# A spectral layer and an MLP on one core: order of the small work in the front, of two spectral stages, and of the residuals

## The chip, the cores and the metric

The kernel runs on one core of one Trainium2 chip. TensorE multiplies matrices into PSUM; VectorE, ScalarE and GpSimd work beside it, each through its own instruction queue in program order; SyncE (SP) issues the DMAs. The metric is the device time of one execution in microseconds, as the median of several runs.

## The reference, cut to what matters

```python
def _layernorm(x, axis=-1, eps=1e-5):
    m = jnp.mean(x, axis=axis, keepdims=True)
    v = jnp.var(x, axis=axis, keepdims=True)
    return (x - m) / jnp.sqrt(v + eps)

# A: x (1, 2048, 512) bf16, w_r and w_i (2048, 257)
X = rfft2(x.astype(float32)) * (w_r + 1j * w_i)
y = irfft2(X, s=(2048, 512)).astype(bfloat16)

# B: w1 (512, 1792), w2 (1792, 512)
h = einsum("bsd,df->bsf", x, w1) + b1
r = where(h > 0, h, 0)
out = einsum("bsf,fd->bsd", r * r, w2) + b2

x = A_x
h = x + A(_layernorm(x), A_w_r, A_w_i)
h2 = h + B(_layernorm(h), B_w1, B_b1, B_w2, B_b2)
```

## The kernel before

The 2048 rows of x lie as 128 partitions by 16 groups (row 16p + g is partition p, group g), a tile of 512 columns for each group. The two-dimensional transform is done with matrix multiplications by tables of sines and cosines that the kernel makes itself: integer angles by `iota` and multiply-add on GpSimd and VectorE, wrapped by reading the low 16 bits, then `Sin` on ScalarE.

*Layer norm and stage 1 (to about 23 us).* The mean drops out and the scale of a row is folded into the table: `ln1_stats(g)` takes BATCH_NORM_STATS2 and BATCH_NORM_AGGREGATE of group g on VectorE (L219, L222); `ln1_sums(g)` does the same for groups 3, 7 and 11 with two ScalarE activations and their accumulator reads (L211); `ln1_rstd(a, b)` makes the reciprocal root on GpSimd, an add and a POW (L225, L226); `ln1_fold(a, b)` multiplies the table KF by it, one VectorE instruction for each group (L230). `stage1(g0)` multiplies two groups by their folded tables (eight matmuls, L247 and L249) and copies the PSUM result into Bt, on ScalarE (L257), or, for the last three pairs (`split`), half on ScalarE and half on VectorE (L254). The optional number in `stage1(g0, n)` is a count of matmuls of ones (`warm`, L262) ahead of it.

*Tables.* fiE[0] holds angles of the second transform (9 x 128), fiE[1] the same plus a quarter turn, made on GpSimd by one instruction of 1152 elements (L286). `table_e(0)` and `table_e(1)` are the sines of both (L198), 9 blocks each, in EF[:, k, 0] and EF[:, k, 1]. fiG (`L282`, `L284`, and `angles_g`, L194) are the angles of stage 2's table GF. The inverse tables EI are transposes of EF blocks: `transposed(o, ks)` (L267) with the identity `ident` as the moving matrix, `table_i` copies them on ScalarE (L274), `table_neg` negates on VectorE (L277). The blocks 0 and 8 and KF are transposed into the free half of the first PSUM tile of the last stage-1 pair (`tr08`). `ident` is made on GpSimd by a MEMSET and an AFFINE_SELECT (L315, L316), behind the second gather.

*Weights of the spectrum.* WB[0] and WB[1] hold w_r and w_i; 9 of 16 row blocks come by plain DMA, the other 7, in reversed order, by an indirect DMA that GpSimd issues (`w_reversed(i)`, L157). The loads of W1, W2, b1 and b2 (L324, on SP) wait until both of these gathers have landed.

*Stages 2 to 4 (23 to 53 us).* The work is done for eight pairs of spectral rows. `stage2(pr)`: eight matmuls with GF (L352), copied by ScalarE into U (L368); the first two pairs go in halves (`stage2_one`, L361). `stage3(pr)`: matmuls of U with EF. Pairs 1, 3, 5 and 7 yield AB (L407, ScalarE), from which VectorE makes X by a sum and a difference (`butterfly`, L416, L417); pairs 2, 4 and 6 (`ON_PE`) do that on TensorE too and yield X directly (L398, ScalarE); pair 0 yields X in two halves (L383). `spectral(pr)`: VectorE multiplies X by the weights (L426), adds and subtracts to Z and M (L431, L432, L441, L443), and does the butterfly of the next pair between. `stage4(pr)`: matmuls of Z or M with EI, copied to T2 (L480, L477, L478). All of stages 1 to 4 share one PSUM pool, tag "mm", of four buffers of two banks.

*Stage 5 and the MLP (from 53 us).* `s5(g)` is the last transform of group g (L555), with a copy of the odd half on ScalarE (L558); `s5b(g)` makes R by an add and a subtract on VectorE (L564, L565); `s6(g)` multiplies R by KI (L574) and VectorE adds the row of x (L575, the residual hs); `s6b(g)` takes the statistics of hs, on VectorE (L589, L590) or ScalarE (L586). After `rstd`, `norm` and the transposes (`transp`, L627, L631, L633) a chunk of two to four groups goes through the MLP: `up` (L672, ReLU L675, square L676) and `down` (L705, bias and residual L709, last group L695). While chunk c is in the MLP, `prep_steps(c + 1)` lists the steps of the next chunk with due times; `run` puts each step into the program after the MLP slot at which its due time is reached. Steps of the same round (s6, s5, s5b, s6b) are due within 0.1 of each other. The PSUM banks of p5, p6 and p7 are three, tag "pp".

At the end `pin` fixes the order on every engine as the program text has it.

Of the kernel before, what the change touches and what calls it, by code (L numbers as in the profile page):

```python
# [15 lines left out]
P = 128  # L16
# [18 lines left out]
def kernel(  # L35
# [120 lines left out]
    def w_reversed(i):  # L156
        return nc.gpsimd.indirect_dma_start(  # L157
            out=WB[i][:, 9:16, :].rearrange("p j l -> p (j l)"), out_offset=None,
            in_=(A_w_r, A_w_i)[i].rearrange("k l -> (k l)").unsqueeze(1), element_offset=9 * Df,
            in_offset=bass.IndirectOffsetOnAxis(ap=idxR[:, 0:1], axis=0))  # L160
# [5 lines left out]
    nc.gpsimd.memset(identW[:], 0.0)  # L166
    nc.gpsimd.affine_select(out=identW[:], in_=identW[:], compare_op=ALU.not_equal,
                            fill=1.0 / WSC, base=0, pattern=[[-1, P]], channel_multiplier=1)

    nc.vector.tensor_single_scalar(pI[:, 1:2], pI[:, 0:1], 3, ALU.arith_shift_right)  # L170
    nc.vector.tensor_single_scalar(pI[:, 2:3], pI[:, 0:1], 7, ALU.bitwise_and)
# [41 lines left out]
    def ln1_stats(*mine):  # L213
        sts = {}
        for k in range(len(mine) + 1):
            if k < len(mine):
                g = mine[k]
                sts[g] = st = fwd.tile([P, 6], FP32, tag="st", bufs=4, name="st")
                nc.vector.bn_stats(st[:], xs[:, g, :])  # L219
            if k > 0:  # L220
                g = mine[k - 1]
                nc.vector.bn_aggr(mv1[:, g, :], sts.pop(g)[:])  # L222
# [5 lines left out]
    def ln1_fold(a, b, eng=nc.vector):  # L228
        for g in range(a, b):
            eng.tensor_scalar(KFr[:, g, :], KF[:], rs1[:, g:g + 1], None, ALU.mult)  # L230
# [45 lines left out]
    def table_neg(ks):  # L276
        nc.vector.tensor_scalar(EI[:, ks[0]:ks[-1] + 1, 2, :], EI[:, ks[0]:ks[-1] + 1, 0, :], -1.0, None, ALU.mult)  # L277

    for g in (3, 7, 11):
        ln1_sums(g)  # L280
    ln1_stats(0, 1)
# [1 line left out]
          "the angles of the first stage first")  # L283
    nc.gpsimd.tensor_scalar(fiG[:, 256:512], idxL[:, 256:512], cols[:, 0:1], float(HT), ALU.mult, ALU.add)  # L284
    ln1_rstd(0, 2)
    nc.gpsimd.tensor_scalar(fiE[1][:], fiE[0][:], 1.0, float(QT), ALU.mult, ALU.add)  # L286
    ln1_stats(2, 4)
    ln1_fold(0, 2)
    stage1(0, 14)
    ln1_stats(5)  # L290
    ln1_rstd(2, 6)
    ln1_stats(6, 8)
    ln1_fold(2, 6)
    gathers = [w_reversed(0)]
    stage1(2, 4)
    stage1(4)
    table_e(1)
    ln1_stats(9)
    ln1_rstd(6, 10)
    ln1_stats(10, 12)  # L300
    ln1_rstd(10, 12)
    angles_g(1)
    ln1_fold(6, 10)
    stage1(6, 3)
    ln1_stats(13)
    ln1_rstd(12, 14)
    sin_of(GF[:].rearrange("p t c -> p (t c)"), fiG[:])
    ln1_fold(10, 12)
    stage1(8)
    ln1_stats(14, 15)  # L310
    nc.vector.tensor_scalar(rs1[:, 14:16], mv1[:, 14:16, 1], EPS, None, ALU.add)
    nc.gpsimd.tensor_tensor(rs1[:, 14:16], rs1[:, 14:16], mhalf[:, 0:2], ALU.pow)
    ln1_fold(12, 14)
    gathers.append(w_reversed(1))
    nc.gpsimd.memset(ident[:], 0.0)  # L315
    nc.gpsimd.affine_select(out=ident[:], in_=ident[:], compare_op=ALU.not_equal,  # L316
                            fill=1.0, base=0, pattern=[[-1, P]], channel_multiplier=1)
    stage1(10, split=True)
    ln1_fold(14, 16)
    for k, (dst, src) in enumerate(((W1[:], B_w1.rearrange("(c p) f -> p c f", p=P)),  # L320
                                    (W2[:], B_w2.rearrange("(i p) d -> p i d", p=P)),
                                    (b1b[:], B_b1.rearrange("(i p) -> p i", p=P)),
# [17 lines left out]

    def cos_negs():
        nc.vector.tensor_scalar(Cn[:], EF[:, ON_PE[0]:ON_PE[-1] + 1:ON_PE[1] - ON_PE[0], 1, :], -1.0, None, ALU.mult)


    GFv = GF[:].rearrange("p t (r e j) -> p t r e j", r=2, e=2)
# [139 lines left out]

    new_u(0)
    new_u(1)
    stage2_one(0, 0, nc.scalar.copy)
    stage2_one(0, 1, nc.vector.tensor_copy)
    stage2_one(1, 0, nc.scalar.copy)  # L490
    nc.vector.tensor_copy(EI[:, 0::8, 0:2, :], tr08[:, 0:4 * P].rearrange("p (a k b) -> p a k b", a=2, k=2))
    cos_negs()
    stage3(0)
    stage2_one(1, 1, nc.scalar.copy)
    stage3(1)
    stage2(2)
    tr = mm_tile("ptr", BF16)
    transposed(tr, (1, 2, 3))
    table_i(tr, (1, 2, 3))
    stage3(2)  # L500
    for pr in range(9):
        if pr + 3 < 8:
            stage2(pr + 3)
        if 0 < pr and pr + 2 < 8:
            stage3(pr + 2)
        if pr == 7:
            warm(mm_tile("idle")[:, 0:512], 3)
        if pr > 0:
            stage4(pr - 1, split=(pr == 8))
        if pr == 8:  # L510
            warm(mm_tile("idle")[:, 0:512], 3)
        if pr == 1:
            table_neg((1, 3))
        if pr == 3:
            table_neg((4, 7))
            nc.vector.tensor_scalar(EN[:].rearrange("p n (k b) -> p n k b", k=2), EI[:, NO_M[0]:NO_M[-1] + 1, 0:2, :],
                                    -1.0, None, ALU.mult)
        if pr == 0:
            spectral(0, first_tables)
        elif pr < 8:  # L520
            spectral(pr)
        if pr == 1:
            tr = mm_tile("ptr", BF16)
            transposed(tr, (4, 5, 6, 7))
            table_i(tr, (4, 5, 6, 7))
        if pr == 5:
            sin_of(GI[:].rearrange("p t c -> p (t c)"), fiI[:])
            nc.gpsimd.tensor_copy(b1f[:], b1b[:])
        if pr == 6:
            nc.scalar.activation(junk1[:], eps[:], ACT.Sqrt, bias=eps[:])  # L530
# [14 lines left out]
    def bank(name, tag, bufs, dt=FP32):  # L545
        return ps.tile([P, 2048 // mybir.dt.size(dt)], dt, tag=tag, name=name, bufs=bufs)

    Rs = {}

    def s5(g, ahead=False):  # L550
        pe = bank("p5", "po", 2) if ahead else bank("p5", "pp", 3)
# [15 lines left out]
    def s6(g):  # L567
        py = bank("p6", "pp", 3)
        if g == 0:
            nc.tensor.matmul(py[:], lhsT=identW[:], rhs=xs[:, 0, :], start=True, stop=False)  # L570
            nc.tensor.matmul(py[:], lhsT=KI[:], rhs=Rs.pop(g)[:], start=False, stop=True)
            nc.scalar.activation(hs[:, 0, :], py[:], ACT.Copy, scale=WSC, accum_out=mv2[:, 0, 0:1])
            return
        nc.tensor.matmul(py[:], lhsT=KI[:], rhs=Rs.pop(g)[:], start=True, stop=True)  # L574
        nc.vector.scalar_tensor_tensor(hs[:, g, :], py[:], WSC, xs[:, g, :], ALU.mult, ALU.add)  # L575

    def s6b(g, on_act=False):
        if g == 0:
# [56 lines left out]
    def prep_steps(c, total):  # L635

        a, b = CHUNKS[c]
        n = b - a
        first = 2 if c == 1 else 0
        end = total - 7.3  # L640
        t0 = 1.2 if c == 1 else total - 0.5 - 2.0 * n - 7.0
        gap = (end - t0) / (n + 1 - first)
        t0 = end - (n + 1) * gap
        steps = []
        for k in range(first, n + 2):
            t = t0 + k * gap
            if k >= 2:
                steps.append((t, 0.22, lambda g=a + k - 2: s6(g)))
            if k < n:
                steps.append((t, 0.44, lambda g=a + k: s5(g)))  # L650
            if 1 <= k <= n:
                steps.append((t + 0.1, 0, lambda g=a + k - 1: s5b(g)))
            if k >= 2:
                steps.append((t + 0.1, 0, lambda g=a + k - 2: s6b(g, on_act(c, g))))
        t = t0 + (n + 1) * gap
        steps.append((t + 1.6, 0, lambda: rstd(c)))
        steps.append((t + 2.2, 0, lambda: norm(c)))
        steps.append((total - 2.4, 0.12 * n, lambda: transp(c, 0)))
        steps.append((total - 1.7, 0.12 * n, lambda: transp(c, 1)))
        return steps  # L660
# [80 lines left out]
    s6(0)  # L741
    s6b(0, True)
    s6(1)
    s6b(1)
    rstd(0)
    norm(0)
# [37 lines left out]
```

## Time and profile before

| what | value |
|---|---|
| median of 14 runs | 179.05 us (177.5 to 180.16) |
| profiled execution: its time, and its span | 177.51 us, 175.7 us |
| granted TensorE clock, mean | 1.000 |
| busy: TensorE, VectorE, ScalarE, GpSimd | 159.0, 127.2, 105.9, 37.2 us |
| last Bt copy of stage 1 ends, stage 2 goes on | 23.18, 23.24 us |
| rows of x landed (groups 0-1, 2-3, 4-7, 8-11, 12-15) | 3.66, 5.18, 6.62, 9.55, 10.81 us |
| gathers landed | 15.50, 23.23 us |

In the profile's lines PE is TensorE, PEld its weight load, DVE VectorE, ACT ScalarE, POOL GpSimd. Times are from the start of the span in microseconds. A line of the chain gives a start, a duration and what was done; the chain is followed back from the last instruction to what released each step. A line of the waits names who waited for whom, the total, the number of times and the longest. In the timeline, an instruction is overlapped by the next of its engine, so a step from one start to the next is shorter than the duration that stands there. The 14 runs lie at three levels, 177.5 (three runs), 178.7 to 179.1 (five) and 180.0 to 180.2 (six).

### The profile page before, as it was taken

The numbers are of one execution on the slowest core, as the hardware profiler recorded it, in microseconds if no ns is written. First come the engines' busy times: TensorE is split into PE (matmuls) and PEld (weight loads), VectorE is DVE, ScalarE is ACT, GpSimd is POOL, SyncE is SP. The second block draws the span as 40 slices with busy tenths as digits, with TensorE's granted clock in tenths as the row PEclk, the third lists the DMA queues.
The fourth block names the chain that finished last, engine by engine and source line by source line (L and its number), as shares of the span: only waits on it lengthen the run. The fifth ranks groups of instructions, "written<-read, shape, count | busy, mean of one in ns | idle before, by whom it ended". The sixth has DMA issues, their size and how long they took to land.

```text
span 175.7 us, 2735 instructions
## 1 busy us (share of the span) xinstructions
PE 159.0 (91%) x995; PEld 92.9 (53%) x995; DVE 127.2 (72%) x297; ACT 105.9 (60%) x184; POOL 37.2 (21%) x65
## 2 busy tenths in 40 slices
PE   3878487999998899989999999999999998999992
PEld 1355355787865476556544544544544453556461
DVE  6999768889975688759888476488757558468231
ACT  3979456899897376078752577454277523568300
POOL 8769740000000000525000054000025200025000
PEclk9999999999999999999999999999999999999999
DMA  5983259940000000010000100000100000010011
GB/s 150 302 299 103 59 147 407 331 34 0 2 0 0 4 0 0 32 35 0 0 0 30 63 0 0 2 30 30 34 30 0 0 30 4 30 60 0 0 50 45
DMA packets 7918, 10.29 MB, mean 59 GB/s; under 512 B 2272, under 2 KB 6368, under 8 KB 7904
## 3 DMA queue, kind: packets, MB, share of 16 engines
q1 hardware_dynamic: 7744, 9.19, 16.8%
q0 software_dynamic: 160, 0.92, 1.8%
q8 instruction: 8, 0.13, 0.3%
q14 instruction: 6, 0.05, 0.1%
HBM read 8.01 MB, written 2.10 MB: 58 GB/s over the span
## 4 chain that ended last, share of the span: by engine, by line
PE 65%; DVE 18%; ACT 7%; POOL 5%; issue 3%; POOLq 0%; ACTq 0%; DVEq 0%
PE ph L672 26%; PE po L705 24%; DVE st L219 2%; PE p L555 2%; DVE KFr L230 2%; PE p L574 2%; DVE hs L575 2%; PE p L627 2%; PE po L693 2%; ACT U L368 2%; POOL rs L226 2%; PE p L352 2%; ACT rl L675 1%; DVE R L564 1%; DVE R L565 1%
## 5 line engine op out<-in xcount | busy, mean ns | idle before, releaser
L672 PE MATMUL ph<-UT,W 128*128 128x384 bf16 (+2 forms) x280 | 49.9, 336 | 1.2 <-ACT UT L631 1.0
L675 ACT ACTIVATE rl<-ph,b1f 128x384 bf16<-128x384 f32 (+2 forms) x70 | 41.5, 602 | 13.9 <-PE ph L672 10.2
L705 PE MATMUL po<-W,act 128*128 128x512 bf16 x210 | 49.1, 379 | 0.0
L676 DVE TENSOR_TENSOR act<-rl 128x384 bf16<-128x384 bf16 (+2 forms) x70 | 34.2, 514 | 16.2 <-ACT rl L675 15.7
L679 POOL TENSOR_TENSOR hb<-hs,b2b 128x512 f32<-128x512 bf16 x16 | 18.4, 1153 | 105.8 <-DVE act L676 105.8
L672 PEld LDWEIGHTS <-W 128*128 128x128 bf16 x280 | 27.4, 98 | 22.6 <-issue 1.7
L705 PEld LDWEIGHTS <-act 128*128 128x128 bf16 x210 | 20.4, 98 | 21.8 <-issue 0.6
L709 DVE TENSOR_TENSOR ot<-po,hb 128x512 bf16<-128x512 f32 x15 | 10.3, 688 | 9.4 <-PE po L705 8.2
L575 DVE SCALAR_TENSOR_TENSOR hs<-p,xs 128x512 bf16<-128x512 f32 x15 | 10.3, 684 | 2.4 <-PE p L574 2.4
L558 ACT COPY od<-p 128x256 f32<-128x256 f32 x16 | 5.9, 371 | 9.1 <-PE p L555 8.9
L631 ACT COPY UT<-p 128x768 bf16<-128x768 bf16 (+2 forms) x5 | 4.2, 842 | 11.0 <-PE p L627 11.0
L262 PE MATMUL p<-ones 128*128 128x512 bf16 x21 | 6.8, 478 | 2.9 <-POOL ones L153 2.9
L555 PE MATMUL p<-GI,T 128*128 128x256 bf16 x64 | 9.1, 272 | 0.2 <-DVE T L478 0.2
L352 PE MATMUL p<-GF,Bt 128*128 128x256 bf16 x64 | 8.3, 273 | 0.5 <-DVE Bt L254 0.3
L555 PEld LDWEIGHTS <-T 128*128 128x128 bf16 x64 | 6.2, 97 | 4.5 <-issue 1.4
L219 DVE BATCH_NORM_STATS2 st<-xs 128x6 f32<-128x512 bf16 x13 | 8.5, 677 | 0.0
L586 ACT ACTIVATE junk<-hs 128x512 bf16<-128x512 bf16 x6 | 3.8, 630 | 7.7 <-DVE hs L575 7.7
L262 PEld LDWEIGHTS <-ones 128*128 128x128 bf16 x39 | 4.2, 109 | 7.6 <-POOL ones L153 2.9
L564 DVE TENSOR_TENSOR R<-p,od 128x256 bf16<-128x256 f32 x16 | 6.7, 416 | 2.1 <-ACT od L558 2.1
L574 PE MATMUL p<-R,KI 128*128 128x512 bf16 x15 | 5.7, 381 | 1.6 <-DVE R L565 1.6
L480 ACT CAST T<-p 128x1024 bf16<-128x1024 f32 x7 | 7.2, 1027 | 0.0
L352 PEld LDWEIGHTS <-Bt 128*128 128x128 bf16 x64 | 6.1, 98 | 1.8 <-ACT Bt L254 0.5
(171 smaller groups left out, 230.9 us busy)
## 6 DMA issues: line engine op xcount, KB each, us to landing
W<-in_B_w_dram SPq DMA_DIRECT2D x2, 1792.0 KB, 9.8
out_dram<-ot SPq DMA_DIRECT2D x15, 128.0 KB, 1.8
xs<-in_A_x_dram SPq DMA_DIRECT2D x3, 512.0 KB, 5.9
WB<-in_A_w_r_dram SPq DMA_DIRECT2D x1, 578.2 KB, 5.8
WB<-in_A_w_i_dram SPq DMA_DIRECT2D x1, 578.2 KB, 6.8
xs<-in_A_x_dram SPq DMA_DIRECT2D x2, 256.0 KB, 3.5
b2b<-in_B_b_dram SPq DMA_DIRECT2D x1, 128.0 KB, 9.2
out_dram<-ot SPq DMA_DIRECT2D x2, 64.0 KB, 1.5
```

The costliest lines, as they stand in the source:

```text
L219: nc.vector.bn_stats(st[:], xs[:, g, :])
L262: nc.tensor.matmul(o, lhsT=ones[:, 0:P], rhs=ones[:], start=True, stop=True)
L352: nc.tensor.matmul(puv[:, :, e, :], lhsT=Bt[:, 2 * t + 1 - e, 2 * pr + q, :], rhs=GFv[:, t, :, e, :], start=(t == 0), stop=(t == 1))
L555: nc.tensor.matmul(pe[:, 256 - 256 * e:512 - 256 * e], lhsT=T2[:, lt, g].rearrange("p q s -> p (q s)"), rhs=GI[:, lt, :], start=(r == 0), ...
L574: nc.tensor.matmul(py[:], lhsT=KI[:], rhs=Rs.pop(g)[:], start=True, stop=True)
L575: nc.vector.scalar_tensor_tensor(hs[:, g, :], py[:], WSC, xs[:, g, :], ALU.mult, ALU.add)
L672: nc.tensor.matmul(ph[:, 0:n], lhsT=W1[:, d, bass.ts(f, P)], rhs=UT[:, d, 0:n], start=(d == 0), stop=(d == ND - 1))
L675: nc.scalar.activation(rl[:, 0:n], ph[:, 0:n], ACT.Relu, bias=b1f[:, f:f + 1], scale=1.0)
L676: sq = nc.vector.tensor_tensor(act[:, f, 0:n], rl[:, 0:n], rl[:, 0:n], ALU.mult)
L679: add = nc.gpsimd.tensor_tensor(hb[:, g, :], hs[:, g, :], b2b[:], ALU.add)
L705: nc.tensor.matmul(po[:], lhsT=act[:, f, bass.ts(i, P)], rhs=W2[:, f, :], start=(f == 0), stop=(f == NF - 1))
L709: nc.vector.tensor_tensor(ot[:], po[:], hb[:, g, :], ALU.add)
```

## The change

1. `ident` is made right behind `identW`, near the start of GpSimd's queue.
2. The quarter-turn angles of fiE[1], one instruction of nine blocks, become two: `angles_c(slice(0, 9, 8))` for the blocks 0 and 8, and `angles_c(slice(1, 8))` for the seven between. Both stand later on GpSimd. `table_e(1)` becomes `table_c` of the same two pieces; the second stands behind the last pair of stage 1.
3. The first gather goes ahead of the first folds; on GpSimd it stands before the first angle piece and `ln1_rstd(2, 6)`.
4. Group 13's statistics go from VectorE to ScalarE (`ln1_sums(13)`, between the copies of pairs 0 and 2). Group 9's statistics go ahead of the folds of groups 2 to 5. The reciprocal roots are taken in groups 0-1, 2-5, 6-9, 10-13 and 14-15 (12 and 13 were on their own). The folds of 14 and 15 go ahead of the pair of groups 10 and 11. The matmuls of ones are 12, 6 and 2 (were 14, 4 and 3).
5. Of the first two halves of stage 2, VectorE copies the first and ScalarE the second (was the other way).
6. Stage 2 of pair 2 is put ahead of stage 3 of pair 1; the transposes of blocks 1 to 3 go behind stage 3 of pair 2; `table_neg((1, 3))` goes behind `spectral(1)`.
7. The residual add of `s6` becomes a step of its own, `s6a`, which is called with `s6b`; so in the rounds of `prep_steps` it stands behind `s5b`.

```diff
+    nc.gpsimd.memset(ident[:], 0.0)
+    nc.gpsimd.affine_select(out=ident[:], in_=ident[:], compare_op=ALU.not_equal,
+                            fill=1.0, base=0, pattern=[[-1, P]], channel_multiplier=1)
...
+    def angles_c(sl):
+        return nc.gpsimd.tensor_scalar(fiE[1][:].rearrange("p (a b) -> p a b", a=9)[:, sl],
+                                       fiE[0][:].rearrange("p (a b) -> p a b", a=9)[:, sl], 1.0, float(QT), ALU.mult,
+                                       ALU.add)
+
+    def table_c(sl):
+        nc.scalar.activation(EF[:, sl, 1, :], fiE[1][:].bitcast(I16)[:, ::2].rearrange("p (a b) -> p a b", a=9)[:, sl],
+                             ACT.Sin, scale=SIN_SCALE)
...
     ln1_rstd(0, 2)
-    nc.gpsimd.tensor_scalar(fiE[1][:], fiE[0][:], 1.0, float(QT), ALU.mult, ALU.add)
+    gathers = [w_reversed(0)]
     ln1_stats(2, 4)
-    ln1_fold(0, 2)
-    stage1(0, 14)
+    f01 = ln1_fold(0, 2)
+    angles_c(slice(0, 9, 8))
+    stage1(0, 12)
+    ln1_sums(13)
     ln1_stats(5)
     ln1_rstd(2, 6)
-    ln1_stats(6, 8)
+    ln1_stats(6, 8, 9)
+    ln1_rstd(6, 10)
     ln1_fold(2, 6)
-    gathers = [w_reversed(0)]
-    stage1(2, 4)
+    stage1(2, 6)
     stage1(4)
-    table_e(1)
-    ln1_stats(9)
-    ln1_rstd(6, 10)
+    table_c(slice(0, 9, 8))
     ln1_stats(10, 12)
-    ln1_rstd(10, 12)
+    ln1_fold(6, 10)
     angles_g(1)
-    ln1_fold(6, 10)
-    stage1(6, 3)
-    ln1_stats(13)
-    ln1_rstd(12, 14)
+    ln1_rstd(10, 14)
+    stage1(6, 2)
     sin_of(GF[:].rearrange("p t c -> p (t c)"), fiG[:])
+    ln1_stats(14)
+    angles_c(slice(1, 8))
     ln1_fold(10, 12)
     stage1(8)
-    ln1_stats(14, 15)
+    ln1_stats(15)
...
     ln1_fold(12, 14)
     gathers.append(w_reversed(1))
-    nc.gpsimd.memset(ident[:], 0.0)
-    nc.gpsimd.affine_select(out=ident[:], in_=ident[:], compare_op=ALU.not_equal,
-                            fill=1.0, base=0, pattern=[[-1, P]], channel_multiplier=1)
+    ln1_fold(14, 16)
     stage1(10, split=True)
-    ln1_fold(14, 16)
...
+    table_c(slice(1, 8))
...
-    stage2_one(0, 0, nc.scalar.copy)
-    stage2_one(0, 1, nc.vector.tensor_copy)
+    stage2_one(0, 0, nc.vector.tensor_copy)
+    stage2_one(0, 1, nc.scalar.copy)
...
     stage2_one(1, 1, nc.scalar.copy)
+    stage2(2)
     stage3(1)
-    stage2(2)
+    stage3(2)
     tr = mm_tile("ptr", BF16)
     transposed(tr, (1, 2, 3))
     table_i(tr, (1, 2, 3))
-    stage3(2)
...
-        if pr == 1:
-            table_neg((1, 3))
...
         if pr == 1:
+            table_neg((1, 3))
...
-        nc.vector.scalar_tensor_tensor(hs[:, g, :], py[:], WSC, xs[:, g, :], ALU.mult, ALU.add)
+        Ys[g] = py
+
+    def s6a(g):
+        nc.vector.scalar_tensor_tensor(hs[:, g, :], Ys.pop(g)[:], WSC, xs[:, g, :], ALU.mult, ALU.add)
...
-                steps.append((t + 0.1, 0, lambda g=a + k - 2: s6b(g, on_act(c, g))))
+                steps.append((t + 0.1, 0, lambda g=a + k - 2: (s6a(g), s6b(g, on_act(c, g)))))
...
     s6(1)
+    s6a(1)
     s6b(1)
```

## The prediction

> **What bounds the kernel now.** I read the table of stretches first (length, then busy time and instruction count of TensorE, its weight loads, VectorE, ScalarE, GpSimd, then the granted clock):
>
> ```profile
> 4.40:23.20 18.80, 13.42 (x88) 8.37 (x86) 16.70 (x49) 13.91 (x25) 14.29 (x27) 1.00 0.57 190
> ...
> 60.60:175.70 115.10, 109.79 (x636) 59.47 (x635) 76.64 (x165) 60.37 (x117) 18.40 (x16) 1.00 0.06 19
> ```
>
> From 60.6 us on TensorE is busy 109.8 of 115.1 us; in layer norm and stage 1 (4.4 to 23.2) only 13.4 of 18.8, and in 23.2 to 35.5 10.7 of 12.3. The clock is 1.00 in every stretch. So the time to win lies before 35.5 us, and behind 60 only in the few gaps of TensorE. The chain that ended last, in order of time, tells what these stretches wait for (start, duration, work):
>
> ```profile
> 20.53 0.57 POOL ident L316
> 21.14 0.38 PE p1a L267 x4
> ...
> 22.49 0.70 DVE Bt L254
> 23.24 1.38 PE p L352 x11
> ...
> 27.51 1.01 ACT AB L407
> 28.52 0.92 ACT U L368
> 29.48 0.38 PE p L390
> ...
> 87.31 0.33 DVE R L564
> 87.64 0.34 DVE R L565
> 88.03 0.38 PE p L574
> ```
>
> Three places: GpSimd makes an identity just when the transposes of the last stage-1 pair need it; the copies of stages 3 and 2 queue on ScalarE before stage 3 of pair 2; and in the MLP a residual (L575) stands on VectorE ahead of the R that TensorE wants. The list of waits prices them (total, times, longest):
>
> ```profile
> PE p1a L267 <- POOL ident L316: 1.3, 1, 1.3
> ...
> PE p L390 <- ACT U L368: 0.8, 1, 0.8
> DVE EI L277 <- ACT EI L274: 0.8, 1, 0.8
> ```
>
> and, of the part behind 60 us:
>
> ```profile
> PE p L574 <- DVE R L565: 1.4, 3, 0.6
> ```
>
> The timeline of GpSimd and VectorE shows a fourth: two folds take 1.24 us beside the angle instruction, four take 0.87 alone. The single rows are 1.05 us for the first, which ends with the angles, against 0.28.
>
> ```profile
> 7.29 1.15 POOL L286 TENSOR_SCALAR fiE<-fiE 128x1152 int32<-128x1152 int32 x1
> 7.47 1.24 DVE L230 TENSOR_SCALAR KFr<-KF,rs 128x256 bf16<-128x256 bf16 x2
> ...
> 11.08 0.87 DVE L230 TENSOR_SCALAR KFr<-KF,rs 128x256 bf16<-128x256 bf16 x4 [0.16 <-POOL rs L226]
> ```
>
> **The change, part by part.** All sums are made against the profiled execution (span 175.7, time 177.51 us). It is the lowest of three levels (177.5, 178.7 to 179.1, 180.0 to 180.2) that the 14 runs show; I know no cause for the levels, and carry the difference over to the median, 179.05.
>
> Identity first. MEMSET 0.22 and AFFINE_SELECT 0.34 (the row of identW, 3.72) go to 4.04 on GpSimd. Behind them stand two column products and two angle pieces, which ended at 5.78 and will end near 6.0; GpSimd then waited until 6.16 for the first statistics anyway. Cost 0; with an AFFINE_SELECT of 0.56 (the other row) 0.1 to 0.2 on the first fold, which has slack below.
>
> Front, first folds. The angles leave 7.29; the first gather (DMA_INDIRECT 1.22, landing 4.3 us after issue) stands there instead, ahead of the angle piece and of rstd(2,6). Beside the gather of 11.24 folds took 0.28, beside that of 19.12 one took 0.44. So folds 0 and 1 end at about 7.95 to 8.1 instead of 8.71. The gain of 0.7 is not kept: VectorE then does statistics 5, 6, waits for rows 8 to 12 (landed 9.55), does 8 and now also 9 (0.60 plus 0.10), and reaches folds 2 to 5 at 11.09; it was 11.08. GpSimd has rs(2,6) by 7.35 + 1.2 + 0.48 (256 angles) + 1.36 (L225, L226) = 10.45, so 0.6 us of cover.
> The Trainium skill (SBUF — State Buffer, "SBUF: two separate sides") says more than these rows: VectorE and GpSimd take a port pair as an exclusive lock for a whole instruction, and descriptors that GpSimd writes for a DMA wait for it. The stretched fold of 7.47 agrees; the four folds beside the gather of 11.24 do not. By the page the gather lands some 0.3 us later, for which nothing waits, and the fold discussed next is held for certain, so that the front gains no more than the lower of its ends below.
>
> Front, VectorE from 11.95: statistics 13 leave it (0.60 + 0.10), 9 is already done, so folds 6 to 9 start at 13.3 instead of 14.35 (angles_g, 2 x 0.48 until 13.65, may hold the first by 0.35). rs(10,14) is one POW of 1.03 and ready at 15.07; in the profile its halves came at 15.41 and 17.59. Against the change: the 896 remaining angles (0.96 us, by the line through 0.48 for 256 and 1.15 for 1152) start on GpSimd at that very POW, just when folds 10 and 11 start. By the row of 7.47 the second fold is held until 16.2 (cost 0.7); by that of 15.97 (0.26) it is not. I take the first, the nearer case. Then statistics 15, L311, folds 12 and 13 end at 17.6 (were 18.56), POW ends at 18.0 (18.94), folds 14 and 15 end at 18.7 (19.75), and, now behind them, the copy of p1b of pair 10 runs at 18.8 to 19.5 (was 18.47).
>
> Front, ScalarE: sums of group 13 (four instructions, 1.48 us start to start as for group 11) come in at 12.0, table_e(1) of 1.18 shrinks to a piece of 0.31 (0.40, overlapped), and the rest (896, 0.95) goes behind stage 1. Step for step 11.97 + 1.48 + 2 x 0.91 + 0.31 + 0.91 (Bt) + 0.96 (GF) + 0.90 = 18.35 for the copy of pair 10, against 18.52: no loss and no gain. Rows 12 to 16 landed at 10.81; the earlier gather moves beside them, worst 10.81 + 2.4 (packets of a gather alone), and 1.2 us late.
>
> Front, end. Without ident the transposes follow stage 1 of pair 12. That pair's p1b waited at 19.21 for a buffer that a VectorE copy gave back; which buffer it gets after the change I can't see. If it needs the copy that ends at 19.5: matmuls 19.55 to 20.15, its copy 20.2 to 20.9, GF and EF (0.16, 0.48) to 21.3, last copy 21.3 to 22.0, stage 2 at 22.05 against 23.24, gain 1.2. If not: 2.1. The identity alone, all else as it was: matmuls from 19.65, copy at 21.0, gain 1.5. I take 1.5. The second gather keeps its place and comes 1 us earlier; on SP the loads of W1, W2 and the biases wait for its landing (23.3) and follow it; their data is used from 60 us. The late table piece ends on ScalarE 0.9 us after the last Bt copy, and ScalarE idled 1.14 there; the first U copy goes to VectorE (0.69 for 0.59), the second to ScalarE: 0.
>
> Stage 2 of pair 2 ahead of stage 3 of pair 1, transposes (1,2,3) behind stage 3 of pair 2, table_neg behind spectral(1). On the old clock: U of pair 2 is copied at 26.9 to 27.9, AB of pair 1 at 27.8 to 28.8 (was 27.51 to 28.52), stage 3 of pair 2 starts at 28.0 instead of 29.48, X at 29.9 (31.42), EI 30.8, U of pairs 3 and 4 at 31.5 and 32.4 (32.34, 33.24), AB of pair 3 at 33.55 (34.46). Gain 0.9. VectorE gets AB of pair 1 0.3 us later, loses the wait of 0.8 for EI, and waits for AB of pair 3 as before (L416, 1.0). Ends: 0 if a buffer binds (TensorE has four, one held by the transposed tables), 1.3 if the waits of 0.5 (L403) and 0.8 (L390) both go.
>
> MLP, s6a behind s5b. R goes ahead of the residual of 0.60. TensorE stood 0.42, 0.36 and 0.59 us for R (88.0, 116.3, 147.2). At the first two the next s5 needs the bank that the residual frees, and that is now later: L555 starts at 88.03 for 88.24 and at 116.31 for 116.53, so 0.2 each; at the third no s5 follows: 0.59. Sum 1.0. Ends: 1.4, and -0.6 if later residuals make the transposes at the end of a chunk wait (their inputs have 0.46, 0.47 and 0.18 us to spare).
>
> Sum: 1.5 + 0.9 + 1.0 = 3.4 us; profiled time 174.1, forecast for the median 175.6.
>
> **Rivals.** (1) Only the identity pays: ScalarE's full queue takes back the reordering, and the delayed residuals the MLP's part. For it: ScalarE is busy 16.9 of 18.0 us from 35.5 on. Against: that stretch shifts as a whole. Gain 1.5 with ends 1.0 and 2.6, 177.5.
> (2) Nothing: the angles at 15.1 hold the folds, rows 12 to 16 land late and ScalarE's chain, with 0.18 us to spare at the start of pair 10's copy, becomes the bound. A landing at 13.2 costs 1.2 us of the 1.5, and the rest hides: about 178.5.
> (3) Slower: TensorE loses its clock in the new wait before pair 2 (10.0 to 11.4; two more warm matmuls, but the folds come no earlier) and gets it back only inside stage 2. Every matmul there doubles; the 10.7 busy us of 23.2 to 35.5 cost up to 10.7 more. It decides when more than 3.4 us of TensorE-bound work is done at half clock; 4.5 us of it give 180.2. Against: the clock stayed 1.00 over a wait of 1.33 (ident).
> The skill (TensorE: Matmul & The Clock Gate, Part 1) puts the drop behind an idle window of about 3.4 us; by it this rival is excluded, and no run here shows a drop.
>
> **How the numbers follow.** Forecast 0.58, rival (1) 0.25, (2) 0.07, (3) 0.04, and 0.06 for mixtures of the losses. 0.5% (0.9 us) is about what a measurement of this kernel tells from no change. Faster holds the forecast, (1) and part of the mixtures, 0.86; same (2), 0.08; slower 0.06. The forecast's own ends are 1.2 + 0.9 + 0.2 = 2.3 and 2.1 + 1.3 + 1.4 = 4.8 us, 174.3 to 176.8; the range reaches to (1) at 177.5 and, for the levels of the runs, down to 173.7.
>
> **What would show it.** Transposes (L267, p1a) at 19.6 to 20.3 with no wait for ident; folds 0 and 1 at 0.3 each; a fold near 15.2 stretched to about 1 us; the first L352 pair complete near 21.1 to 22.0; AB of pair 3 at 31.1 to 32.4; the L574 waits for R gone. Wrong it would be if x's last rows land after 13, if L416 or L390 wait longer, if new waits of L555 for the residual or of the chunk transposes for u appear, or if the clock row falls below 1.

## The result and the profile after

| | before | after |
|---|---|---|
| median of the runs compared | 177.61 us (47 runs, 177.5 to 180.3) | 176.61 us (10 runs, 175.01 to 178.67) |
| lowest level, clock 1.00 throughout | 177.5 us | 175.0 to 175.3 us |
| profiled execution: time, span, mean granted clock | 177.51, 175.7, 1.00 | 178.25, 175.5, 0.981 |

After stands to before as 0.985, with a 95% interval of 0.9797 to 0.9903. The runs of one kernel lie at levels, because in some executions the granted TensorE clock is lost for a while; the profiled execution of the changed kernel is one of those, so its lines can be read against the old ones only up to the place where the clock falls. At full clock the change is worth 2.2 to 2.5 us (2.5 by the spans, 175.7 and 173.2). In the medians it is worth 1.0, because in these runs the changed kernel lost the clock more often: in 8 of the 12 executions whose clock is on record, against 22 of the 47 runs of before, those above 178.5 us. That share varies by itself: in the sets of before that ran beside the experiments below it was 2 of 11, 17 of 29 and 5 of 11.

The table of stretches of the changed kernel (length; busy time and count of TensorE, its weight loads, VectorE, ScalarE, GpSimd; clock; DMA share and rate) shows where:

```profile
4.40:23.20 18.80, 13.95 (x86) 8.61 (x84) 14.98 (x46) 14.35 (x30) 14.70 (x27) 0.89 0.55 186
23.20:35.50 12.30, 10.86 (x79) 7.50 (x78) 9.74 (x22) 8.62 (x13) 0.00 (x0) 0.88 1.00 303
...
60.00:175.50 115.50, 110.44 (x645) 60.06 (x644) 78.54 (x170) 60.91 (x118) 18.41 (x16) 1.00 0.06 19
```

The clock column was 1.00 in every stretch before; now it is 0.89 and 0.88 ahead of 35.5 us. The clock records put it exactly: 1.00 from 5.55 to 19.21 us, 0.50 from 19.21 to 26.03, then 1.00 again. The last Bt copies and the first half of stage 2 fall into that time, and in the chain (start, duration, work) their matmuls take about 1.6 times as long:

```profile
18.57 0.61 DVE Bt L257
19.22 0.37 PE p1b L250
...
20.27 0.70 DVE Bt L257
21.02 0.61 PE p1a L270 x4
...
23.48 0.70 DVE Bt L257
24.23 2.23 PE p L363 x11
```

Four transposes take 0.61 us (0.38 before), eleven matmuls of stage 2 2.23 (1.38 before). But there are also two waits for copies by VectorE, the first of them over just as the clock fell. The list of waits ahead of 60 us (who waited for whom, total, times, longest):

```profile
PE p1b L250 <- DVE Bt L257: 1.0, 1, 1.0
...
PE p1a L270 <- DVE Bt L257: 0.8, 1, 0.8
DVE X L427 <- ACT AB L418: 0.7, 1, 0.7
...
PE p L413 <- ACT U L379: 0.6, 1, 0.6
```

The wait of 1.3 us for `ident` is gone. In its place the transposes (L270, p1a) wait for VectorE's copy of p1b of pair 12, behind the wait of p1b of pair 12 for VectorE's copy of pair 10. VectorE's wait of 0.8 for EI is gone. Behind 60 us the list of TensorE's waits has one line for the inverse stages:

```profile
PE p L565 <- DVE hs L588: 0.2, 1, 0.2
```

The three waits of s6's matmul for R, 1.4 us in all, are gone; s5 waits once for the delayed residual.

The timelines of VectorE and GpSimd (start, duration, instruction) hold the two places at which the prediction was specific about folds:

```profile
7.43 0.50 DVE L233 TENSOR_SCALAR KFr<-KF,rs 128x256 bf16<-128x256 bf16 x2
...
15.10 1.16 DVE L233 TENSOR_SCALAR KFr<-KF,rs 128x256 bf16<-128x256 bf16 x2 [0.42 <-POOL rs L229]
```

```profile
7.47 1.23 POOL L157 DMA_INDIRECT WB<-in_A_w_r_dram,idxR  x1 [0.21 <-issue]
...
15.15 1.03 POOL L283 TENSOR_SCALAR fiE<-fiE 128x896 int32<-128x896 int32 x1
```

The first two folds no longer stand beside angles and take 0.50 us instead of 1.24. Folds 10 and 11 now do, and take 1.16.

### The profile page after: what moved, and what is told of

Read it like the earlier page. It is cut to its first block, busy times and chain, and to the rows that moved or that the text cites. A ratio compares the mean times of both kernels' runs of the same rounds, so it can differ in the third digit from the quotient of the medians.

```text
span 175.5 us, 2735 instructions
## 1 busy us (share of the span) xinstructions
PE 160.4 (91%) x994; PEld 93.6 (53%) x994; DVE 126.6 (72%) x295; ACT 107.1 (61%) x189; POOL 36.8 (21%) x64
## 2 busy tenths in 40 slices
DMA packets 7917, 10.27 MB, mean 59 GB/s; under 512 B 2272, under 2 KB 6368, under 8 KB 7904
## 4 chain that ended last, share of the span: by engine, by line
PE 70%; DVE 13%; ACT 8%; DMA 5%; issue 2%; POOL 1%; ACTq 0%; DVEq 0%
PE ph L685 28%; PE po L718 24%; DMA xs<-in_A_x_dram 5%; PE p L363 3%; PE p L565 3%; PE p L640 2%; PE po L706 2%; ACT junk L214 2%; ACT U L379 2%; PE p L584 1%; DVE Bt L257 1%; DVE hs L588 1%; DVE mA L437 1%; DVE mB L437 1%; ACT Bt L260 1%
## 5 line engine op out<-in xcount | busy, mean ns | idle before, releaser
L689 DVE TENSOR_TENSOR act<-rl 128x384 bf16<-128x384 bf16 (+2 forms) x70 | 34.2, 515 | 16.2 <-ACT rl L688 15.7
L363 PE MATMUL p<-GF,Bt 128*128 128x256 bf16 x64 | 9.1, 294 | 0.6 <-DVE Bt L257 0.6
L565 PE MATMUL p<-GI,T 128*128 128x256 bf16 x64 | 9.1, 272 | 0.6 <-DVE T L489 0.2
L265 PE MATMUL p<-ones 128*128 128x512 bf16 x20 | 6.1, 458 | 2.9 <-POOL ones L153 2.9
L565 PEld LDWEIGHTS <-T 128*128 128x128 bf16 x64 | 6.2, 98 | 3.9 <-issue 0.9
L574 DVE TENSOR_TENSOR R<-p,od 128x256 bf16<-128x256 f32 x16 | 6.6, 414 | 2.1 <-ACT od L568 2.1
L222 DVE BATCH_NORM_STATS2 st<-xs 128x6 f32<-128x512 bf16 x12 | 7.8, 675 | 0.0
L575 DVE TENSOR_TENSOR R<-p,od 128x256 bf16<-128x256 f32 x16 | 6.6, 414 | 0.0
```

The costliest lines, as they stand in the source:

```text
L265: nc.tensor.matmul(o, lhsT=ones[:, 0:P], rhs=ones[:], start=True, stop=True)
L363: nc.tensor.matmul(puv[:, :, e, :], lhsT=Bt[:, 2 * t + 1 - e, 2 * pr + q, :], rhs=GFv[:, t, :, e, :], start=(t == 0), stop=(t == 1))
L565: nc.tensor.matmul(pe[:, 256 - 256 * e:512 - 256 * e], lhsT=T2[:, lt, g].rearrange("p q s -> p (q s)"), rhs=GI[:, lt, :], start=(r == 0), ...
L689: sq = nc.vector.tensor_tensor(act[:, f, 0:n], rl[:, 0:n], rl[:, 0:n], ALU.mult)
```

## The experiments

Two questions were open: what the lost clock costs and what causes it (theory 1: TensorE's short waits ahead of stage 2 together, and the levels of both kernels are this; rival: the levels have another cause), and where the front's gain went (theory 2: to the buffers of the divided stage-1 tiles; rival: to the clock alone, or the rearranged front gives nothing). All kernels compute the whole reference. Those that were run together share their runs of before; the medians of before in the three sets were 177.5 (11 runs), 178.73 (29) and 177.54 (11), with a level of 177.5 in each. "At full clock" below means executions with a mean granted clock of 0.996 or more.

### The changed kernel again

> The changed kernel as it is, for a profile with TensorE's clock undisturbed and for the spread of its runs. In the profile at hand the granted clock was one half from 19.2 to 26.0 us (mean 0.981). Theory 1: the runs differ by how many stretches of 3.41 us the clock is halved; with none the time is 175.0 to 175.3, with one 176.2 to 177.5, with two 177.7 to 178.7. Theory 2: in the front the gain is only 0.5 to 0.7 of the 1.5 us predicted, because the last pair of stage 1 now waits for a PSUM buffer that VectorE's copy of the pair before frees (0.8 us in the profile at hand): with the full clock, stage 2 goes on at 22.6 to 22.8 instead of 23.24. Rival to 2: without the halved clock that wait is gone and stage 2 goes on at 21.7 or earlier, so that the loss lies behind 23 us.

Six runs: 175.08 at clock 1.00; 176.13 to 176.23, four runs, at 0.99; 177.99 at 0.981, the profiled one. Ratio 0.9898 (0.986 to 0.9936). Its clock stood at 0.50 from 20.36 to 27.18 us. A mean clock of 0.99 is one halved stretch of 3.41 us, 0.98 two; they cost 1.1 and 2.9 us of the time here, 1.1 to 1.2 and 2.7 of the span. Theory 1's reading of the levels fits. On theory 2 the profile tells less, since stage 2 fell into the halved clock again (it goes on at 23.82 us). But the transposes' wait of 0.8 began at 19.82 here, ahead of the fall, so it isn't made by the clock.

### One PSUM buffer for each of pairs 10 and 12

```diff
-            two = [mm_tile("p1a"), mm_tile("p1b")]
-            pts = [pt[:, 0:512] for pt in two]
+            two = [mm_tile("p1a"), mm_tile("p1b")] if pre else [mm_tile("p1a")]
+            pts = [pt[:, 0:512] for pt in two] if pre else [two[0][:, 0:512], two[0][:, 512:1024]]
...
-            return two[0][:, 512:1024].bitcast(BF16)
+            return two[0][:, 512:1024].bitcast(BF16) if pre else None
```

> The changed kernel, but the pairs of groups 10-11 and 12-13 take one PSUM buffer each (both halves of it) instead of two buffers of which half is used. Theory 2 (buffers): the waits of p1b for VectorE's copy (1.0) and of the transposes for VectorE's copy (0.8) go, stage 2 goes on at 20.9 to 21.3 instead of 22.7, and the time with the full clock falls by 1.2 to 1.7 us against the changed kernel, to 173.4 to 174.0. Rival (queues): VectorE's copies stand behind the folds of groups 14 and 15 anyway, stage 2 goes on at 22.2 or later, gain under 0.5 us.

Median 173.5 us (173.38 to 173.74, six runs), clock 0.996 or more in all; ratio 0.9762 (0.9729 to 0.9795). The chain of this kernel:

```profile
19.31 0.69 DVE Bt L257
20.00 0.08 DVE GF L339
20.08 0.39 DVE EF L340
20.47 0.60 DVE Bt L257
21.07 0.05 issue
21.12 1.37 PE p L363 x11
```

No transposes and no p1b matmuls stand in it any more: VectorE's copies follow each other, and stage 2 goes on at 21.12. At full clock that is 1.5 us better than the changed kernel. Theory 2 holds. The built programs say why. The tile pool gives out its four buffers when the program is built, and in the changed kernel p1b of pair 10, p1b of pair 12 and p1a of the last pair lie in the same two PSUM banks, one after another; each must wait for VectorE's copy of the one before.

### The changed kernel with ten matmuls of ones

```diff
+            if fill[t]:
+                warm(two[t][:, 512:1024], fill[t])
...
-    stage1(10, split=True)
+    stage1(10, split=True, fill=(0, 2))
...
-    stage1(12, split=True)
+    stage1(12, split=True, fill=(4, 4))
```

> The changed kernel with ten more matmuls of ones, two behind the pair of groups 10-11, four between the halves of the pair of 12-13 and four behind it, all into the unused halves of those buffers, in stretches in which TensorE only waits (1.0 and 0.8 us). Theory 1 (work in a stretch sets the clock): no run has a halved clock any more, all lie at 175.0 to 175.4, median 175.2. Rival (the halving has another cause, such as the chip's power or a fixed chance): the same mix of clocks 1.00, 0.99 and 0.98 as for the changed kernel, median 176 to 177.

Median 174.91 us (174.89 to 175.01), clock 0.998 or more in all six runs; ratio 0.984 (0.9807 to 0.9873). The ones hold the clock, and the time is that of the undisturbed runs of the changed kernel, or 0.1 to 0.4 better. Its chain:

```profile
18.57 0.61 DVE Bt L259
19.18 0.04 issue
19.22 0.27 PE p1b L250
...
19.82 0.88 PE p1b L267 x4
20.69 0.02 issue
20.72 0.69 DVE Bt L259
...
22.57 0.05 issue
22.62 1.38 PE p L365 x11
```

Even with the clock held stage 2 goes on only 0.62 us earlier than before (23.24), so the clock alone is not where the front's gain went. It is not the changed kernel plus a clock, though: here p1a of the last pair got a buffer of its own, and in exchange the copy at 20.72 waits for the four ones in its tile.

### One buffer and ones

```diff
-    stage1(10, split=True)
+    stage1(10, 2, split=True)
...
-    stage1(12, split=True)
+    stage1(12, 3, split=True)
...
-    tr08 = stage1(14, split=True, pre=lambda o: transposed(o, (0, 8), True))
+    tr08 = stage1(14, 4, split=True, pre=lambda o: transposed(o, (0, 8), True))
```

> One buffer for each of the two pairs, as in the kernel before this in the list, and two, three and four matmuls of ones ahead of the pairs of groups 10-11, 12-13 and 14-15. If both theories hold: clock 1.00 in all runs and 173.4 to 174.0 us in the median. If only the buffers hold: fastest runs at 173.4 to 174.0, others 1.2 and 2.4 us above. If the matmuls of ones get in the way of the data (each takes 0.22 us): 0.2 to 0.6 us above the one with the buffers alone, at the full clock.

Median 173.73 us (173.73 to 173.82), ratio 0.9774 (0.9741 to 0.9806). Where the waits are gone the ones buy nothing and cost 0.2: stage 2 at 21.45 instead of 21.12.

### The residual back ahead of R

```diff
-                steps.append((t, 0.22, lambda g=a + k - 2: s6(g)))
+                steps.append((t, 0.22, lambda g=a + k - 2: (s6(g), s6a(g))))
...
-                steps.append((t + 0.1, 0, lambda g=a + k - 2: (s6a(g), s6b(g, on_act(c, g)))))
+                steps.append((t + 0.1, 0, lambda g=a + k - 2: s6b(g, on_act(c, g))))
```

> The changed kernel with the residual back in its old place ahead of R in the rounds of the MLP; all else as changed. As predicted for that part: 1.0 us slower than the changed kernel at the full clock (176.0 to 176.3 against 175.0 to 175.3), the three waits of L584 for R (0.42, 0.36, 0.59 us) come back, the new wait of the next s5 for a bank (0.20) goes. Rival (the delayed residuals cost as much elsewhere): within 0.3 us of the changed kernel.

At full clock 176.08 to 176.40 us (six runs; a seventh 177.82); all twelve have a median of 176.83, ratio 0.9924 (0.989 to 0.9959). Against 175.0 to 175.3 the residual's place is worth 1.0 to 1.1. TensorE's waits behind 60 us in this kernel begin with the line that the change had removed:

```profile
PE p L584 <- DVE R L575: 1.4, 3, 0.6
```

### The old order of stages 2 and 3

```diff
-    stage2(2)
     stage3(1)
-    stage3(2)
+    stage2(2)
     tr = mm_tile("ptr", BF16)
     transposed(tr, (1, 2, 3))
     table_i(tr, (1, 2, 3))
+    stage3(2)
...
+        if pr == 1:
+            table_neg((1, 3))
...
         if pr == 1:
-            table_neg((1, 3))
```

> The changed kernel with stage 3 of pair 1 ahead of stage 2 of pair 2 again, the transposes of blocks 1 to 3 ahead of stage 3 of pair 2, and their negation ahead of the spectral step of pair 1; all else as changed. As predicted for that part: 0.9 us slower than the changed kernel at the full clock (175.9 to 176.2). Rival (buffers or ScalarE's queue took the reordering back): within 0.3 us.

Five runs at full clock, 175.8, 176.11, 176.15, 176.49 and 177.07; median of all twelve 177.03, ratio 0.9898 (0.9848 to 0.9948). By the lowest runs, and by the middle of each set, the order is worth 0.8 to 1.0 us. The waits of VectorE bring back the one for EI:

```profile
DVE EI L280 <- ACT EI L277: 0.8, 1, 0.8
```

### Before, with the identity first and nothing else

```diff
+    nc.gpsimd.memset(ident[:], 0.0)
+    nc.gpsimd.affine_select(out=ident[:], in_=ident[:], compare_op=ALU.not_equal,
+                            fill=1.0, base=0, pattern=[[-1, P]], channel_multiplier=1)
...
-    nc.gpsimd.memset(ident[:], 0.0)
-    nc.gpsimd.affine_select(out=ident[:], in_=ident[:], compare_op=ALU.not_equal,
-                            fill=1.0, base=0, pattern=[[-1, P]], channel_multiplier=1)
```

> The kernel before with nothing changed but the identity made at the start. As worked out in the prediction: transposes right behind the pair of groups 12-13, stage 2 goes on at 21.75 instead of 23.24, 1.5 us faster than before at the full clock (176.0). Rival: a buffer wait takes its place here too (the transposes wait for VectorE's copy that ended at 20.53), gain 0.5 us or less. If the identity alone gives more than the whole front of the changed kernel, the other changes in the front cost the difference.

Median 176.08 us (176.06 to 176.16), clock 0.998 or more in all six; ratio 0.9905 (0.987 to 0.9941). At full clock the gain is 1.43, and the chain shows it as the prediction had worked it out for the identity alone:

```profile
19.25 0.27 PE p1b L250
...
19.89 0.69 DVE Bt L257
20.58 0.08 DVE GF L330
20.66 0.39 DVE EF L331
21.05 0.69 DVE Bt L257
21.74 0.05 issue
21.79 1.37 PE p L352 x11
```

Here p1b of pair 12 waits for VectorE's copy of pair 10 as well, but p1a of the last pair lies in other banks and waits for nothing. So the rest of the front's rearrangement made the changed kernel's front worse than this, not better: 22.62 or later against 21.79.

### Before, with the same ten matmuls of ones

The edit is that of the changed kernel with ones.

> The kernel before with the same ten matmuls of ones in the same places of stage 1. Theory 1 (the levels of the kernel before are halved clocks too): its three levels 177.5, 178.7 to 179.1 and 180.0 to 180.2 become one, 177.5 to 177.7. Rival (the levels of the kernel before have another cause): its levels stay, in about the same shares.

Twelve runs, 177.49 to 177.61 us, clock 0.997 or more in all. Of the 29 runs of before beside them 17 were at 0.98 or 0.99, with 178.7 to 180.3 us. Ratio 0.9974 (0.9948 to 1.0). Ten matmuls that compute nothing leave the lowest level where it is and take the two others away. The levels of before are the same lost clock.

### One buffer, with the front in the old order

The kernel with one buffer, with the instructions from the first `ln1_rstd` to the folds of groups 14 and 15 and the table of fiE[1] in the order of before (items 2 to 4 of the change undone, the identity still first):

```diff
     ln1_rstd(0, 2)
-    gathers = [w_reversed(0)]
+    nc.gpsimd.tensor_scalar(fiE[1][:], fiE[0][:], 1.0, float(QT), ALU.mult, ALU.add)
     ln1_stats(2, 4)
...
     gathers.append(w_reversed(1))
-    ln1_fold(14, 16)
     stage1(10, split=True)
+    ln1_fold(14, 16)
```

> One buffer for each of the two split pairs, stages 2 and 3 and the residuals as in the changed kernel, but the front in the order of the kernel before, with only the identity made at the start. If the rearranged front (angles, gather, statistics, folds) is worth something once the buffers are out of its way: stage 2 goes on at 21.7 to 21.8 instead of 21.12, time 174.0 to 174.1 against 173.4 to 173.7. Rival (it is worth nothing): 173.4 to 173.7. If it costs: under 173.3.

Median 174.55 us (174.47 to 174.55), ratio 0.9786 (0.9722 to 0.9851), stage 2 at 22.18. With the buffers out of the way, the rearranged front is worth 1.05 us, more than the 0.6 expected. One reason is in VectorE's timeline:

```profile
19.21 0.69 DVE L257 CAST Bt<-p1a 128x512 bf16<-128x512 f32 x1 [0.59 <-ACT Bt L257]
```

ScalarE and VectorE each copy half of the shared tile, and the program makes VectorE wait until ScalarE has ended. In this order ScalarE is late with it. That is a price of one buffer for two halves, and it makes the comparison a little unfair to the old front.

### The long angles behind the second gather

```diff
-    angles_c(slice(1, 8))
     ln1_fold(10, 12)
...
     gathers.append(w_reversed(1))
+    angles_c(slice(1, 8))
     ln1_fold(14, 16)
```

> The kernel with one buffer for each of the two split pairs, but the 896 angles stand on GpSimd behind the second gather instead of beside folds 10 and 11. If the held fold is on the path: folds 10 and 11 take 0.48 instead of 1.16 us, folds, copies and stage 2 come 0.4 to 0.9 us earlier (stage 2 at 20.2 to 20.75; the later end if the negation of EF is now the one that is held), time 172.5 to 173.1. Rival (ScalarE's chain binds in its place): within 0.2 us of 173.4 to 173.7.

Median 173.17 us (172.94 to 173.6), ratio 0.9712 (0.9647 to 0.9777): 0.3 better than one buffer alone by the medians, less than was expected (172.5 to 173.1). The two sets of runs overlap (173.38 to 173.74 there), and stage 2 goes on at 20.91 for 21.12. VectorE's timeline:

```profile
15.10 0.48 DVE L233 TENSOR_SCALAR KFr<-KF,rs 128x256 bf16<-128x256 bf16 x2 [0.42 <-POOL rs L229]
...
18.47 1.29 DVE L257 CAST Bt<-p1a 128x512 bf16<-128x512 f32 x2 [0.57 <-ACT Bt L257]
```

The folds lose the 0.68 us that the angles had cost them (1.16 to 0.48). Most of it ends in the next wait, 0.57 for ScalarE's copy of the shared tile: the rival is right for the larger part.

### The sign change of EF behind the last copy

```diff
-    nc.vector.tensor_scalar(EF[:, :, 2, :], EF[:, :, 0, :], -1.0, None, ALU.mult)
     tr08 = stage1(14, split=True, pre=lambda o: transposed(o, (0, 8), True))
+    nc.vector.tensor_scalar(EF[:, :, 2, :], EF[:, :, 0, :], -1.0, None, ALU.mult)
```

This stands on top of the edit before it.

> As the kernel with the late angles, and VectorE negates EF behind the last copy of stage 1 instead of ahead of it. If the negation, held by the angles or not, stands on the path: 0.3 to 0.7 us faster than the kernel with the late angles, 172.2 to 172.6. Rival (TensorE or ScalarE end last there): within 0.2 us of it.

Median 172.84 us; ratio 0.9702 (0.9633 to 0.977). Four runs lie at 172.65 to 172.87 and two at 173.94 and 173.99. Of these two the profiled one ended its last VectorE instruction at 168.12 us, earlier than the kernel before it (168.67), but its span is 172.2 for 171.4: the last part of the output landed at 171.0 us, 1.3 behind the others. Whether the edit has a part in that is not shown; the other four runs don't have it. Stage 2 goes on at 20.36, 0.55 earlier than in the kernel before it, and the median is 0.3 lower: the negation stood on the path. This is the best version: 4.7 us under before where both have their clock, about twice what the change itself gives.

### The identity first, with seven ones fewer early on

The kernel with the identity first, less the four and the three matmuls of ones ahead of pairs 2 and 6:

```diff
-    stage1(2, 4)
+    stage1(2)
...
-    stage1(6, 3)
+    stage1(6)
```

> The kernel before with the identity at the start (six runs at 176.06 to 176.16, no halved clock), and without the seven matmuls of ones ahead of the pairs of groups 2-3 and 6-7, which no data waits for. Theory 1 (work in a stretch of 3.41 us sets the clock): some runs now show a halved clock (mean 0.99 or 0.98) and lie 0.5 to 2.5 us higher; those with the full clock stay at 176.1. Rival: all at 176.1 and clock 1.00.

Median 176.07 us (176.07 to 176.2), clock 0.997 or more in all six runs; ratio 0.9876 (0.9811 to 0.9942). The list of TensorE's waits ahead of 25 us begins with

```profile
PE p L250 <- DVE KFr L233: 4.1, 3, 1.8
```

Waits of up to 1.8 us, longer than any of the changed kernel's, and no clock lost. In some of these runs theory 1 had forecast a lost clock, and that missed: the length of a wait doesn't decide. Counted from where this kernel's own clock came up, 6.14 us, its first four stretches of 3.41 us held 2.44, 1.62, 2.04 and 2.27 us of TensorE's work; what that says of the theory stands in the next section.

### What takes the clock

The clock records of four profiles have a fall ahead of 60 us, and all agree on a grid: the clock falls 13.65 us, four times 3.41, after it came up, and stays down for one or two times 3.41. When it comes up differs between executions (5.55 to 7.85 us). The busy time of TensorE in the stretch just ahead of the fall, and in the halved stretches, can be read from tables of stretches. The changed kernel's:

```profile
15.79:19.20 3.41, 1.46 (x11) 0.90 (x10) 2.88 (x9) 2.89 (x4) 2.06 (x3) 1.00 0.00 0
19.20:22.62 3.42, 2.61 (x15) 1.70 (x15) 1.21 (x3) 0.00 (x0) 2.87 (x8) 0.50 0.45 139
22.62:26.03 3.41, 2.84 (x14) 1.69 (x13) 1.64 (x4) 1.53 (x3) 0.00 (x0) 0.50 0.73 194
26.03:29.44 3.41, 3.41 (x26) 2.37 (x25) 2.32 (x5) 2.88 (x5) 0.00 (x0) 1.00 1.02 407
```

That with the old order of stages 2 and 3, which lost one stretch:

```profile
18.09:21.50 3.41, 1.61 (x17) 1.12 (x15) 2.24 (x6) 0.83 (x2) 3.12 (x7) 1.00 0.42 118
21.50:24.92 3.42, 2.97 (x16) 1.65 (x14) 1.73 (x4) 1.62 (x3) 0.71 (x2) 0.50 0.46 88
```

And that of before, profiled without a fall, whose clock came up at 6.41 us:

```profile
16.65:20.06 3.41, 2.02 (x16) 1.29 (x14) 3.28 (x11) 3.06 (x5) 2.48 (x4) 1.00 0.01 2
20.06:23.48 3.42, 1.84 (x17) 1.28 (x17) 1.64 (x4) 0.59 (x1) 3.14 (x10) 1.00 0.48 139
```

The stretch ahead of a fall held 1.46 and 1.61 us of TensorE's work here, and 1.38 and 1.52 in the changed kernel run again and with the residual back; stretches with 1.84 and 2.02 kept the clock. So the line lies near half of the stretch. The clock came back after halved stretches with 2.84 and 2.97 us of work (and 3.23 and 3.37 in the two others) and not after 2.61 and 2.64. It is not one long wait that costs the clock but the sum of the idle time in a stretch whose place is chance. The ten ones raise the stretch of before from 2.02 to 2.80, and the kernel with one buffer has 2.44 where the changed one has 1.46.

The records say more at the end of the executions, where TensorE runs out of work. With the late negation the clock fell at 169.91 us, after a stretch with 1.18 us of work, and with seven ones fewer at 173.39, after one with 1.12. With one buffer and the old front a stretch of 1.62 us, from 167.87 us on, kept it, and so did the one of 1.62 us from 9.55 us on with seven ones fewer, the wait of 1.8 us within it. So the fourth stretch is no rule of its own: in the four profiles the thin part of the front lies there, and at the end the fall came after 48 and 49 stretches.

By these readings the line for a fall lies at 1.61 to 1.62 us of 3.41. That is finer than the profile can tell, since the ends of its matmuls are modelled; "near 1.6" is safe. The limits were read from the records and not tried by an experiment of their own.

## Why the prediction was right, and where it was not

The sign was right, and the median of 176.61 us lies in the range of 173.7 to 177.5. The forecast for it was 175.6; in terms of the profiled level, 174.1 against 175.0 to 175.3 measured. The forecast's 3.4 us became 2.2 to 2.5 at full clock, the low end of its own sum (2.3), and 1.0 in the medians, below that end. That the median still lies in the range is partly luck: the range was reckoned down from a median of 179.05 for before, which was 177.61 in the runs compared. By size alone rival (1), with its 1.0 to 2.6 us, fits as well; only the experiments decide against it. The ends of the sum were also taken too narrowly: 0.9 and 0.2 stand in the low one where the terms' own ends were 0 and -0.6. By its terms:

**Front, first folds.** Right. The angles had held them: beside the gather they take 0.50 us, beside the angles they took 1.24, and folds 2 to 5 start at 10.71 instead of 11.08, about where they were. The identity early on costs nothing that shows. Two slips change nothing: the four folds of 0.87 that the prediction first calls alone stood beside the gather of 11.24, as it says itself further on, and its sum for rs(2,6) gives 10.39, not 10.45.

**Front, from 11.95.** Right. The 896 angles hold the second of folds 10 and 11 until 16.2, the dearer of the two cases weighed. Moving them away freed 0.68 us on VectorE, but the next wait stood behind it, and 0.2 to 0.3 was left.

**Front, end.** This is the step that failed: 1.5 taken, with ends 1.2 and 2.1. Its first half came out: p1b of pair 12 got the buffer of VectorE's copy of pair 10, the case priced at 1.2, and because that copy ended at 19.18 and not 19.5 it would have been worth about 1.5. What it left out is that p1a of the last pair could land in the same buffer once more. At full clock this puts the copy of pair 12 (19.85 to 20.55), the transposes and the last pair's matmuls one behind the other instead of side by side, with stage 2 at an estimated 22.75: 20.55, transposes of 0.46 with the one of KF, two rows of matmuls of 0.43, a copy of 0.70 and some 0.2 between them. The gain is then 0.5. Measured: 0.62 with the clock held by ones, and 2.2 to 2.5 less the two other terms (1.8 to 2.1), 0.1 to 0.7. The text said "which buffer it gets after the change I can't see" of one tile; its range should have allowed the same for the next one. The identity alone brought 1.43, as worked out (1.5): the rearranged front, as its buffers fell, took 0.8 to 1.0 of that away, and is worth 1.05 when each pair has one buffer (in the comparison that is a little unfair to the old front).

**Stage 2 of pair 2 ahead of stage 3 of pair 1.** Right: 0.9 forecast, 0.8 to 1.0 measured by undoing it. The wait of VectorE for EI went, as said; the wait for AB of pair 3, expected to stay at 1.0, fell to 0.7.

**MLP.** Right, and to the size: 1.0 forecast, 1.0 to 1.1 measured. Of the two waits of 0.2 that were to take the place of the first two, one shows (L565, 88.92 to 89.13 us).

**Rivals.** Of (1), only the identity pays, the opposite happened: the two parts it held to be lost paid in full, and the identity's own gain went in part. Of (2) only the held folds came, which the forecast had taken too: the last rows of x landed at 10.27 us, earlier than before. Rival (3), the clock, named the right mechanism with the wrong place and price. It looked for one wait long enough, ahead of pair 2, and held against it that the clock stayed over a wait of 1.33 us. No single wait does it, and the waits that count stand from 16 to 21 us. The price is 1.1 to 1.3 us of the span for one stretch of 3.41, not the doubling of all of stage 2. It does not make the change slower, because before loses its clock too. But it hid more than half of the gain from the median, and it is the cause of the levels for which the prediction had none.

**The signs.** Of what the prediction called signs of being wrong two appeared: the clock row fell to 0.89 and 0.88, which belongs to rival (3), and s5 waited for the residual (L565, 0.2 us), which its own sum for the MLP had counted. The step that failed shows in what it expected to see, the first matmuls of stage 2 complete near 21.1 to 22.0 us: stage 2 goes on at 24.23 in the profile, and at 22.62 with the clock held by ones.

**The rule weighed.** The Trainium skill (TensorE: Matmul & The Clock Gate, Part 1) has the clock go down after an idle window of about 3.4 us, and the prediction excluded rival (3) by it. The runs agree with its length of the window, 3.41, and with its saying that the window runs free of the kernel's start. They do not agree with idle as the condition: the longest wait in the changed kernel's stretch was 1.0 us, and 1.46 of 3.41 us were busy. The skill's other rule (SBUF — State Buffer, "SBUF: two separate sides"), the exclusive lock, which the page has for certain VectorE operations and not for all, fits the folds beside angles, 1.16 us against 0.48, and not the two beside the gather, 0.50. What the prediction drew from it, that the front gains no more than the lower end of 1.2, came true, but mainly through the buffer: moving the angles away gave 0.2 to 0.3 us.

## What to carry to other kernels

Removing a wait shows what stood behind it: before pricing the gain, write down which buffer each of the next tiles will get, for every tile up to the end of the stage, and bound each one that is not known. When run times lie at a few fixed levels, read the granted clock of the runs before anything else, and add up the idle time of TensorE over stretches of 3.41 us rather than looking for one long wait. A few matmuls of ones in the gaps tell within one experiment whether the levels are the clock; taking the waits away is better, and then the ones cost time.

## What the runs showed of the hardware

- The clock went down with no wait longer than 1.0 us, after a stretch of 3.41 us with 1.38 to 1.61 us of TensorE work, and came back after a halved stretch with 2.84 us or more (not after 2.61 and 2.64). It stayed over a wait of 1.8 us in a stretch with 1.62 us of work. One halved stretch cost the changed kernel 1.1 to 1.3 us of the span (174.3 to 174.5 against 173.2), two cost 2.3 to 3.7 (175.5 to 176.9).
- Executions of one program differ mainly in where the stretches lie: 175.0 to 178.7 us for the changed kernel, and 177.49 to 177.61 in all twelve runs of before with ones. Besides, the time was 1.8 to 3.0 us above the span in the changed kernel's executions; no run tells why.
- The first gather, issued at 7.47 us while the rows of x were still on their way, landed 7.5 us later; before, issued at 11.24, it took 4.3. Its early place gained 0.6 us at the landing (14.93 against 15.50) and not the 3.8 of its issue. The rows of x were not held up by it: the last landed at 10.27, before at 10.81.
- A VectorE fold beside GpSimd's angles took 1.05 us in before's rows and a pair 1.16 in the changed kernel's; moved away from them the pair took 0.48. Beside the gather's instruction two folds took 0.50, so that instruction did not hold them.
